# DeltaNet and SwiGLU block: shorter unread products on TensorE, and GpSimd takes part in scaling a mask and spreading Z

## The chip, the cores and the metric

The kernel runs on one core of a Trainium2 chip. Its engines are TensorE (PE, with its weight loads PEld), VectorE (DVE), ScalarE (ACT), GpSimd (POOL) and SyncE (SP, which here issues nearly all DMAs). [...] The metric is the device time of one execution in microseconds; lower is better.

## What is computed

The reference has two parts. The first is a delta-rule recurrence over 768 steps for 4 batches of 8 heads with head size 48. The second is a gated feed-forward layer on its output.

```python
k_n = k / (np.linalg.norm(k, axis=-1, keepdims=True) + 1e-06)
for t in range(S):
    kt, vt, bt = (k_n[:, :, t], v[:, :, t], beta[:, :, t, None])
    y[:, :, t] = np.einsum('bhd,bhde->bhe', q[:, :, t], state)
    v_old = np.einsum('bhde,bhd->bhe', state, kt)
    state = state + bt[:, :, :, None] * np.einsum('bhd,bhe->bhde', kt, vt - v_old)
...
x = np.ascontiguousarray(attn_out.transpose(0, 2, 1, 3)).reshape(B * S, H * D)
g = x @ w_gate
silu = g * (1.0 / (1.0 + np.exp(-g)))
val = x @ w_val
return (silu * val @ w_out).astype(np.float32)
```

w_gate and w_val are 384x1536, w_out is 1536x384; the three come in as 64-bit floats, which the kernel converts to 32 bits itself.

## The kernel before

**Chunks.** The 768 steps are cut into 12 chunks of 64. Inside a chunk the recurrence becomes products: a Gram matrix of K, a unit triangular matrix built from it and from beta, and that matrix's inverse applied to V. Then follow the output of the chunk (through a masked product of Q and K) and the new state. The feed-forward layer for a chunk runs on TensorE while the next chunk's recurrence is prepared beside it. From about 130 us on this is a steady stream of large products. The opening before it is different, since there is nothing yet to hide the recurrence behind.

**The opening.** The body of the kernel is written inside a block that fixes, for PE, ACT, DVE, SP and POOL, the order of the instructions to that in which they are written. Its first part (from L1635) is a list of calls, each of which emits instructions for several engines:

- norms(0), norms(1) on DVE, and the loads of K, Q and V by SP.
- unread(5) (L633): five products of 32 columns of weights with a moving operand of 512 columns, whose result nobody reads. A product in 32-bit floats is two passes in the trace.
- turned(0, ...) transposes K of chunk 0 through TensorE, first_gram makes its Gram matrix, first_diag copies the diagonal blocks into the tile mb on ScalarE; the same then for chunk 1.
- DVE transposes these blocks (L1655); first_scale (L679) multiplies beta and scales the 16x16 masks of both halves with it: POOL makes the factor nb, DVE multiplies the mask (L688).
- stage(n) for n = 0 to 22 fetches pieces of the weights, see below.
- first_substitution (L692): 15 steps on DVE, each a product and a sum. Step j reads row j of the mask: zb[j] times mb[j], added to the rows behind it.
- first_z (L712) transposes the result into Z. spread_z(c, x, engine, heads) (L717) copies Z of chunk c into the padded tile zt, times a mask of rows m_rows. For chunk 0 there are three such copies ahead of the next step: x = 1 for heads 0 to 7 on ScalarE, x = 0 for all heads on DVE, x = 1 for heads 8 to 15 on DVE.
- scale_v(0) and the second halves of the Q Gram steps (a mask multiplied on DVE).
- small_unread(56) (L639) and warm(1) (L646): 56 products of one column and one product of 512 columns, none of them read.
- step("advance", advance, 0): n_products(0) makes N on TensorE from zt and the lower blocks l_sb. Its products go through the heads in the order of every(): the first is of par 0, the second of par 1. A product of par 1 reads zt of heads 8 to 15. Then n_copy (ScalarE), the products p_u with V, and three rounds of correction with N.
- after that the conversion of the weights and the first feed-forward products.

**The staging of weights.** stage(n, after) emits two things. If `after` is given, POOL copies one column of piece `after` into the place of piece n. Then SP issues the DMA of piece n, which overwrites that column:

```python
if after is not None:
    nc.gpsimd.tensor_copy(place[:, 0:1], staged[after][:, 0:1])
queue.dma_start(
    out=place, in_=src[t * 128 : (t + 1) * 128, f0 : f0 + m].bitcast(U32)
)
```

So POOL's copy waits until piece `after` has landed, and SP's DMA waits for POOL's copy: only two or three pieces are under way at a time. The calls stand in this order around the spreads (L1657 to L1681):

```python
for n in range(12):
    stage(n, n - 2 if n > 1 else None)
load_v(1)
stage(12, 10)
stage(13, 11)
...
first_substitution()
for n in range(14, 18):
    stage(n, n - 3)
first_z()
for n in range(18, 23):
    stage(n, n - 3)
```

Of the kernel before, what the change touches and what calls it, by code (L numbers as in the profile page):

```python
# [10 lines left out]
ALU = mybir.AluOpType  # L11
# [4 lines left out]
R = 32  # L16
# [4 lines left out]
def kernel(  # L21
# [25 lines left out]
    nc = tc.nc  # L47
# [21 lines left out]
    def ps_pair(name, tag):  # L69

        return psum.tile([128, 2, 512], FP32, name=name, tag=tag, bufs=1)
# [70 lines left out]
    def load_k(c, dmas=(nc.sync,)):  # L142
        load_heads(kn_of(c), k, c, dmas)

    def load_q(c):
        load_heads(qpad[c % QB], q, c)
# [163 lines left out]
    half = const.tile([128, R], FP32, name="half")  # L310
# [7 lines left out]
    for b in range(2):  # L318
        rows = mask_q[64 * b : 64 * b + 64]
        nc.gpsimd.affine_select(  # L320
            out=rows,
# [35 lines left out]
    def new_n(g):  # L357

        n_t[g] = work.tile([128, 2, HH], FP32, name="n_t")
# [58 lines left out]
    def load_beta():  # L418
        for s_ in range(2):
            for par in range(2):  # L420
                at = beta_rows(s_).start + 8 * par
                nc.gpsimd.dma_start(
                    out=beta_s[at : at + 8],
                    in_=beta.rearrange(
                        "(b bp) (j par) s -> b par (bp j) s", b=2, par=2
                    )[s_ ^ par, par],
                )
# [119 lines left out]
    def gram(*args):  # L547
        for _ in gram_steps(*args):
            pass
# [51 lines left out]
    B16 = R // 2  # L601

    def pairs_of_blocks(flat):

        v = flat.rearrange("p (b n) -> p b n", b=2)[:, :, 0 : B16 * R]
        return v.rearrange("p b (k i) -> p b k i", i=R)
# [23 lines left out]
        )  # L630
        nc.vector.tensor_scalar_mul(m_low, m_rows[:, 0:3], -1.0)

    def unread(count):  # L633

        p = ps_pair("p_t", "px")[:, 0]
        for _ in range(count):
            nc.tensor.matmul(p[0:R], half, half[:, 0:1].to_broadcast([128, 512]))  # L637

    def small_unread(count):  # L639

        p = ps_pair("p_t", "px")[:, 0]
        for n in range(count):
            q_ = QUADS[n % 4][0]
            nc.tensor.matmul(p[q_, 0:1], half[q_], half[q_, 0:1])

    def warm(count):  # L646

        p = ps_pair("p_t", "px")[:, 0]
        for _ in range(count):
            nc.tensor.matmul(p, ident, kts[0][:, 0:512])  # L650
# [15 lines left out]
    def first_diag(c, p):  # L666
        to = first_of["diag"][:, HH * c : HH * c + HH]
        nc.scalar.copy(to.rearrange("p (par h) j -> p par h j", par=2), p[:, :, 1])
# [10 lines left out]
    def first_scale(r_b):  # L679
        zb, b = first_of["zb"], beta_b[:, 0]  # L680
        nb = work.tile([128, R], FP32, name="nb", tag="nb_1", bufs=1)
        for _ in range(2):
            nc.gpsimd.tensor_tensor(out=b, in0=b, in1=r_b, op=ALU.mult)
        nc.gpsimd.tensor_scalar_mul(nb, b, -1.0)
        nc.gpsimd.tensor_copy(zb[:, 0 : R * R : R + 1], b)
        mb = pairs_of_blocks(first_of["mb"])[:, :, :, 0:B16]
        nb = nb.rearrange("p (b i) -> p b i", b=2)[:, :, None, :]
        nc.vector.tensor_tensor(  # L688
            out=mb, in0=mb, in1=nb.to_broadcast([128, 2, B16, B16]), op=ALU.mult
        )  # L690

    def first_substitution():  # L692

# [23 lines left out]
    def spread_z(c, x, engine, heads=slice(0, HH)):  # L717

        z_v = first_of["z"].rearrange("p i (c h) -> p c h i", c=2)[:, c, heads]
        out = ztp[0][:, c, heads, R * x : R * x + R]  # L720
        mask = m_rows[:, 1:2] if x else m_rows[:, 3:4]
        if engine is nc.scalar:
            nc.scalar.mul(out, z_v, mask)
        else:
            nc.vector.tensor_scalar_mul(out, z_v, mask)

    def n_products(c, p_n, pars):

# [14 lines left out]
    def new_nt(c, flat):  # L743
        n_sb[c] = flat.rearrange("p (par bp j i) -> p par bp j i", bp=NB, par=2, j=NJ)
# [5 lines left out]
    QUADS = [(slice(R * n, R * n + R), R * (n % 2)) for n in range(4)]  # L750
# [875 lines left out]
    with tc.manual_schedule(  # L1626
        engines={
            mybir.EngineType.PE,
            mybir.EngineType.Activation,
            mybir.EngineType.DVE,  # L1630
            mybir.EngineType.SP,
            mybir.EngineType.Pool,
        }
    ):
        new_n(0)  # L1635
        load_beta()
        first_tiles()
        norms(0)
        norms(1)
        load_q(0)  # L1640
        load_k(2)
        load_k(3)
        load_q(1)
        load_v(0)
        copy_a = nc.scalar.copy
        unread(5)
        turned(0, False, 0)
        p_g = [first_gram(0, "px")]
        first_diag(0, p_g[0])
        turned(1, False, 2)  # L1650
        spread_beta(copy_a)
        p_g.append(first_gram(1, "py"))
        first_diag(1, p_g[1])
        r_b = first_n()
        nc.vector.transpose(first_of["mb"][:, 0 : R * R], first_of["flat"])  # L1655
        first_scale(r_b)
# [5 lines that stand above are left out]
        low_copies(0, p_g[0])  # L1662
        turned(0, True, 0)
        low_copies(1, p_g[1])
        turned(2, False, "px")
        first_q = [gram_steps(0, True, 2)]
        next(first_q[0])
        turned(3, False, "py")
        turned(1, True, 0)
        gram(2, False, "px", (copy_a, copy_a))  # L1670
        gram(3, False, "py", (copy_a, copy_a))
        first_q.append(gram_steps(1, True, 0))
        next(first_q[1])
        for n in (0, 2):
            power_step(n)
# [6 lines that stand above are left out]
        some, others = slice(0, HH // 2), slice(HH // 2, HH)  # L1682
        spread_z(0, 1, nc.scalar, some)
        spread_z(0, 0, nc.vector)
        spread_z(0, 1, nc.vector, others)
        scale_v(0)
        for steps_of in first_q:
            next(steps_of)
        small_unread(56)
        warm(1)  # L1690
        new_nt(0, qpad[1].rearrange("p bp h d -> p (bp h d)"))
        zb_1 = work.tile([128, R, R], FP32, name="zb", bufs=1)
        new_nt(1, zb_1.rearrange("p k i -> p (k i)"))
        step("advance", advance, 0)
        for x in range(2):
            spread_z(1, x, nc.scalar)
        for n in (4, 1, 3, 5, 6, 7):
            power_step(n)
        for _ in range(6):
            step("advance", advance, 0)  # L1700
        converts_first(0)
        step("advance", advance, 0)
        converts_first(2)
        p_n = banks("p_n", "px")
        n_products(1, p_n, (0,))
        step("advance", advance, 0)
        converts_first(4)
        n_products(1, p_n, (1,))
        converts_first(1, 3)
        converts_first(5)  # L1710
        scale_v(1)
        for par in range(2):
            n_copy(1, p_n, par)

        def chain(at):

            step("advance", advance, 0 if steps("advance", 0) < 4 else 1)
            converts(1 + (at + 1) % 2)

        pairs = [(c, f) for c in range(2) for f in range(0, 8, 2)]  # L1720
        pairs += [(c, f) for f in range(8, FT, 2) for c in range(2)]
        for at, (c, f) in enumerate(pairs):
            early = c == 0 and f < 4
            if c == 1 and f == 0:
                finish(1)
                second_inverse.append(invert(1))
                for _ in range(3):
                    next(second_inverse[0])
            elif not early:
                point(2)  # L1730
            need((6, 12, 18, 24, 30, 30)[f // 2])
            gate_val(c, f, fill, at, chain if early else None)
        need(len(pieces))
        for bp in range(NB):
            point(2)
            output(0, bp, fill, (4, 8))
        output(1, 0, fill, (4, 8))
        hold.clear()
        first_blocks(True)
        first_blocks(False)  # L1740
        point(2)
        output(1, 1, fill, range(2, FT, 2))
        finish(2)
        x_sums(2)
        sums_of_w(12)
        for c in range(2, NCH):
            if c > FAST:
                begin(c, 0)
            point(c + 1)
            if c == FAST:  # L1750
                begin(c, 0)
            for r in range(ROUNDS):
                gate_val_fast(c, r, fill)
            output_fast(c, fill)
            finish(c + 1)
            x_sums(c + 1)
# [30 lines left out]
```

## Time and profile before

| | |
|---|---|
| median of three runs | 697.36 us (696.71 to 699.23) |
| the profiled execution's own time | 697.91 us |
| its span | 696.2 us |
| mean granted TensorE clock | 0.994 |
| idle time of TensorE in the span | 12 us |

The profile is of one execution. A row gives the start, the busy time, the engine, the line of the kernel, the operation, what it writes and reads, and how many instructions were merged into the row. The bracket at its end is the time that the engine sat idle before it, and what ended that idle time. SPq rows are DMAs as SyncE issues them. A few stretches of the opening, as a table of busy time in us:

| us | PE | DVE | ACT | POOL | granted clock |
|---|---|---|---|---|---|
| 1.03 to 7.65 | 6.62 | 4.11 | 1.49 | 4.34 | 1.00 |
| 20 to 25 | 4.83 | 4.45 | 4.04 | 0.20 | 1.00 |
| 26 to 27 | 0.17 | 0.90 | 0.78 | 0.00 | 1.00 |
| 30 to 31 | 1.00 | 1.00 | 0.00 | 0.00 | 0.50 |
| 36 to 40 | 4.00 | 2.22 | 4.00 | 0.55 | 1.00 |
| 46 to 70 | 23.89 | 19.33 | 13.98 | 1.67 | 1.00 |

### The profile page before, as it was taken

To read this page: it belongs to the slowest core of one execution; us is meant where nothing else is said; L and a number is where in the kernel's file an instruction comes from. 1 tells how busy PE (TensorE), PEld (TensorE's weight loads), DVE (VectorE), ACT (ScalarE), POOL (GpSimd) and SP (SyncE) were. 2 spreads that over 40 slices of the span, in tenths; PEclk is the share of its full clock that TensorE was granted. 3 is DMA by queue.
4 is the path that set the end of the run, shared out by engine and by line. 5 is a ranking of instruction groups with operands and counts; after the bars stand their busy time and mean duration, and the time that the engine had idled before them with its cause. 6 is when DMAs were issued, how large, how long until landed. Compare 5 with 4: busy or idle time off the path is not lost.

```text
span 696.2 us, 25657 instructions
## 1 busy us (share of the span) xinstructions
PE 684.1 (98%) x11380; PEld 638.6 (92%) x11380; DVE 473.2 (68%) x1103; ACT 259.4 (37%) x542; POOL 53.3 (8%) x62
## 2 busy tenths in 40 slices
PE   8899999999999999999999999999999999999997
PEld 4688888757999999999999999999999999999997
DVE  6877778897899758886459786389844345333342
ACT  3675765214442532344233244242153142142230
POOL 5000031105000020000300002100000000000000
PEclk9899999999999999999999999999999999999999
DMA  9667824017450621464423373143141231121210
GB/s 133 152 166 196 256 74 154 1 38 176 126 111 13 115 80 40 102 114 85 93 72 71 70 137 70 56 108 70 55 108 48 56 84 46 55 63 46 69 47 23
DMA packets 143854, 62.31 MB, mean 90 GB/s; under 512 B 122976, under 2 KB 126048, under 8 KB 143744
## 3 DMA queue, kind: packets, MB, share of 16 engines
q1 hardware_dynamic: 141536, 60.19, 36.8%
q8 instruction: 89, 1.46, 0.8%
q10 hardware_dynamic: 2080, 0.39, 0.4%
q0 software_dynamic: 128, 0.10, 0.1%
q14 instruction: 21, 0.17, 0.1%
HBM read 53.58 MB, written 7.08 MB: 87 GB/s over the span
## 4 chain that ended last, share of the span: by engine, by line
PE 96%; ACT 1%; issue 1%; DVE 1%; ACTq 0%; DVEq 0%
PE ffn L1180 43%; PE ffn L1386 20%; PE ffn L1276 9%; PE ffn L1303 4%; PE p_g L513 3%; PE p_u L944 2%; PE p_s L1012 2%; PE p_r L905 2%; PE p_y L914 2%; PE p_y L1000 1%; PE p_f L1073 1%; PE p_t L637 1%; PE ffn L964 1%; PE p_u L964 1%; PE p_j L868 1%
## 5 line engine op out<-in xcount | busy, mean ns | idle before, releaser
L1180 PE MATMUL ffn<-x_ffn,wg_sb 128*128 128x128 f32 x840 | 128.3, 275 | 0.3 <-ACT ffn L1236 0.2
L1180 PE MATMUL ffn<-x_ffn,wv_sb 128*128 128x128 f32 x840 | 128.1, 275 | 0.0
L1180 PEld LDWEIGHTS ffn<-x_ffn,wg_sb 128*128 128x128 f32 x840 | 111.1, 192 | 0.6 <-ACT ffn L1236 0.3
L1180 PEld LDWEIGHTS ffn<-x_ffn,wv_sb 128*128 128x128 f32 x840 | 110.7, 192 | 0.0
L1210 ACT ACTIVATE sil<-ffn 128x256 f32<-128x256 f32 x120 | 46.1, 384 | 131.8 <-PE ffn L1180 127.1
L1386 PE MATMUL ffn<-wo_sb,h_f 128*128 128x192 f32 x480 | 83.4, 327 | 0.0
L1215 DVE TENSOR_TENSOR h_f<-sil,ffn 128x256 f32<-128x256 f32 x120 | 49.6, 418 | 47.6 <-ACT sil L1210 45.2
L1386 PEld LDWEIGHTS ffn<-wo_sb,h_f 128*128 128x128 f32 x480 | 78.1, 190 | 0.4
L1347 DVE TENSOR_TENSOR ffn<-ffn,p_sb 128x512 f32<-128x512 f32 x58 | 40.3, 696 | 44.3 <-ACT ffn L1236 43.2
L1180 PE MATMUL ffn<-x_t,h_f 128*128 128x128 f32 x480 | 61.1, 280 | 0.0
L1180 PEld LDWEIGHTS ffn<-x_t,h_f 128*128 128x128 f32 x480 | 56.2, 191 | 1.3 <-ACT ffn L1193 0.2
L591 DVE TENSOR_TENSOR zb<-zb,tmp 128x31 f32<-128x31 f32 (+15 forms) x155 | 53.1, 343 | 5.3
L585 DVE TENSOR_TENSOR tmp<-zb,mb 128x31 f32<-128x31 f32 (+15 forms) x155 | 52.7, 340 | 4.0
L813 POOL TENSOR_TENSOR n_b<-mb,half 128x32 f32<-128x32 f32 x5 | 30.0, 6000 | 289.8 <-DVE mb L555 289.8
L1347 DVE TENSOR_TENSOR o_sb<-o_sb,ffn 128x192 f32<-128x192 f32 x49 | 17.2, 351 | 51.1 <-PE ffn L1386 49.0
L1193 ACT COPY ffn<-ffn 128x512 f32<-128x512 f32 x30 | 17.1, 571 | 63.7 <-PE ffn L1180 57.3
L1386 PE MATMUL ffn<-last_k,h_f 128*128 128x192 f32 x200 | 35.9, 327 | 0.0
L1276 PE MATMUL ffn<-x_ffn,wg_sb 128*128 128x256 f32 x144 | 34.3, 384 | 0.0
L1276 PE MATMUL ffn<-x_ffn,wv_sb 128*128 128x256 f32 x144 | 33.8, 382 | 0.0
L1386 PEld LDWEIGHTS ffn<-last_k,h_f 128*128 128x128 f32 x200 | 32.9, 190 | 0.0
L1276 PEld LDWEIGHTS ffn<-x_ffn,wv_sb 128*128 128x128 f32 x144 | 27.0, 190 | 3.7
L1276 PEld LDWEIGHTS ffn<-x_ffn,wg_sb 128*128 128x128 f32 x144 | 26.6, 190 | 4.1 <-DVE wg_sb L304 0.4
(291 smaller groups left out, 1070.3 us busy)
## 6 DMA issues: line engine op xcount, KB each, us to landing
h_f<-w_s SPq DMA_DIRECT2D x60, 256.0 KB, 2.8
p_sb<-w_s SPq DMA_DIRECT2D x27, 256.0 KB, 2.7
vin<-in_v_dram SPq DMA_DIRECT2D x48, 96.0 KB, 3.3
out_dram<-o_sb SPq DMA_DIRECT2D x48, 96.0 KB, 2.2
kn<-in_k_dram SPq DMA_DIRECT2D x20, 192.0 KB, 4.6
zt<-in_moe_w_out_dram SPq DMA_DIRECT2D x6, 384.0 KB, 4.3
qpad<-in_q_dram SPq DMA_DIRECT2D x36, 64.0 KB, 3.2
w_s<-h_f SPq DMA_DIRECT2D x7, 256.0 KB, 3.6
```

Of the source, the lines that this page charges most:

```text
L513: nc.tensor.matmul(p_v[par][half_of(b if of_q else b ^ par), bp, j], kt[c][half_of(par), bp, j, b], xt[half_of(par), bp, j, b],)
L585: nc.vector.tensor_tensor(out=t_v, in0=zb[:, 0 : j + 1, j : j + 1].to_broadcast([128, j + 1, m]), in1=mb[:, j : j + 1, j + 1 : R].to_broad ...
L591: nc.vector.tensor_tensor(out=zb[:, 0 : j + 1, j + 1 : R], in0=zb[:, 0 : j + 1, j + 1 : R], in1=t_v, op=ALU.add,)
L813: nc.gpsimd.tensor_tensor(out=n, in0=mb.rearrange("p j i -> p (j i)")[:, 0 : R * R : R + 1], in1=half, op=ALU.pow,)
L1180: nc.tensor.matmul(p[:, u], w(u), moving, start=start and u == 0, stop=True, skip_group_check=True,)
L1193: nc.scalar.copy(p_y, p_x)
L1210: nc.scalar.activation(sil[:, n].rearrange("p (i n) -> p i n", i=2), p[:, 0:2], ACTF.Silu)
L1215: nc.vector.tensor_tensor(out=h_of(c, f, j), in0=sil[:, n].rearrange("p (i n) -> p i n", i=2), in1=p[:, 2:4], op=ALU.mult,)
L1276: nc.tensor.matmul(ps[name][:, i], w_sb[:, t, (f + i) * 128 : (f + i + 1) * 128], xts[c][:, t], start=(t == 0 and i == 0), stop=(t == KT - 1),
L1303: nc.tensor.matmul(p_o, hs[c, f - f % 2][:, f % 2, bp * 128 : (bp + 1) * 128], wo_sb[:, f], start=(f == 0), stop=(f == FT - 1),)
L1347: nc.vector.tensor_tensor(out=out, in0=a, in1=b, op=ALU.add)
L1386: nc.tensor.matmul(p[x, part], a(f - f % 2)[:, f % 2], b(f), start=not begun and f == 0, stop=f == FH - 1, skip_group_check=True,)
```

## The change

The opening's five unread products of 512 columns become three, of 512, 512 and 256 columns. The 56 unread products of one column before N go, and the warming product there becomes two. In first_scale the multiplication of the mask is cut by rows: DVE takes rows 0 to 3, GpSimd rows 4 to 15. The third spread of Z for chunk 0 (x = 1, heads 8 to 15) goes from DVE to GpSimd, at the same place of the written order.

```diff
-    def unread(count):
+    def unread(*sizes):
 
         p = ps_pair("p_t", "px")[:, 0]
-        for _ in range(count):
-            nc.tensor.matmul(p[0:R], half, half[:, 0:1].to_broadcast([128, 512]))
-
-    def small_unread(count):
-
-        p = ps_pair("p_t", "px")[:, 0]
-        for n in range(count):
-            q_ = QUADS[n % 4][0]
-            nc.tensor.matmul(p[q_, 0:1], half[q_], half[q_, 0:1])
+        for n in sizes:
+            nc.tensor.matmul(p[0:R, 0:n], half, half[:, 0:1].to_broadcast([128, n]))
...
         mb = pairs_of_blocks(first_of["mb"])[:, :, :, 0:B16]
         nb = nb.rearrange("p (b i) -> p b i", b=2)[:, :, None, :]
-        nc.vector.tensor_tensor(
-            out=mb, in0=mb, in1=nb.to_broadcast([128, 2, B16, B16]), op=ALU.mult
-        )
+        for engine, lo, hi in ((nc.vector, 0, 4), (nc.gpsimd, 4, B16)):
+            engine.tensor_tensor(
+                out=mb[:, :, lo:hi],
+                in0=mb[:, :, lo:hi],
+                in1=nb.to_broadcast([128, 2, hi - lo, B16]),
+                op=ALU.mult,
+            )
...
         if engine is nc.scalar:
             nc.scalar.mul(out, z_v, mask)
         else:
-            nc.vector.tensor_scalar_mul(out, z_v, mask)
+            engine.tensor_scalar_mul(out, z_v, mask)
...
         copy_a = nc.scalar.copy
-        unread(5)
+        unread(512, 512, 256)
         turned(0, False, 0)
...
         spread_z(0, 1, nc.scalar, some)
         spread_z(0, 0, nc.vector)
-        spread_z(0, 1, nc.vector, others)
+        spread_z(0, 1, nc.gpsimd, others)
         scale_v(0)
         for steps_of in first_q:
             next(steps_of)
-        small_unread(56)
-        warm(1)
+        warm(2)
```

## The prediction

> **What bounds the kernel now.** I read the page first. Its busy line says that TensorE sets the time; the other engines matter where TensorE waits for them.
>
> ```profile
> PE 684.1 (98%) x11380; PEld 638.6 (92%) x11380; DVE 473.2 (68%) x1103; ACT 259.4 (37%) x542; POOL 53.3 (8%) x62
> ```
>
> Of 696.2 us TensorE is idle for 12, so an edit off its path is worth nothing, and a wait put in its path costs its full length unless some of those 12 us come back. All edits lie before 31 us, so I read the chain of waits there next (start, length, what).
>
> ```profile
> 1.03 6.62 PE p_t L637 x10
> 26.17 1.49 issue
> 27.67 1.02 PE p_t L644 x82
> 28.73 1.59 PE p_t L650 x2
> 30.32 1.05 PE p_n L734 x28
> ```
>
> The chain opens with the unread products (L637), and just before the first products of N (p_n, L734) it runs through 56 small unread products (L644) and one warming product (L650, two passes). What N truly needs is the VectorE chain beside it. The timelines of VectorE, ScalarE and TensorE:
>
> ```profile
> 16.98 1.25 DVE L1655 STREAM_TRANSPOSE wo_sb<-mb 128x1024 f32<-128x1024 f32 x1 [2.27 <-ACT mb L668]
> 18.32 0.69 DVE L688 TENSOR_TENSOR wo_sb<-wo_sb,nb 128x512 f32<-128x512 f32 x1
> 27.79 1.25 DVE L714 STREAM_TRANSPOSE mb<-zt 128x1024 f32<-128x1024 f32 x1
> 29.07 1.05 DVE L725 TENSOR_SCALAR zt<-mb,m_rows 128x512 f32<-128x512 f32 x2
> 29.07 0.80 ACT L723 ACTIVATE zt<-mb,m_rows 128x256 f32<-128x256 f32 x1 [0.43 <-DVE mb L714]
> 30.25 2.49 PE L734 MATMUL p_n<-zt,a_sb 64*64 64x64 f32 x62
> ```
>
> Mask scaled (L688), 15 substitution steps, a transpose, then three spreads of Z: VectorE's end at 29.07 + 1.05 = 30.12, ScalarE's at 29.87, and N starts at 30.25.
>
> The change gives the last spread to POOL, so I asked what POOL does at 29 us. Its timeline (start, busy time, operation, idle time before it and who ended that), five of its copies of one column:
>
> ```profile
> 24.57 0.20 POOL L254 COPY h_f<-h_f 128x1 uint32<-128x1 uint32 x1 [8.55 <-DMA h_f<-in_moe_w_gate_dram]
> 29.12 0.70 POOL L254 COPY h_f<-h_f 128x1 uint32<-128x1 uint32 x1 [0.96 <-DMA h_f<-in_moe_w_val_dram]
> 43.68 0.18 POOL L254 COPY wo_sb<-wo_sb 128x1 uint32<-128x1 uint32 x1 [3.08 <-DMA wo_sb<-in_moe_w_gate_dram]
> 54.43 0.20 POOL L254 COPY wo_sb<-wo_sb 128x1 uint32<-128x1 uint32 x1 [4.27 <-DMA wo_sb<-in_moe_w_gate_dram]
> 60.21 0.18 POOL L254 COPY zt<-wo_sb 128x1 uint32<-128x1 uint32 x1 [0.98 <-DMA wo_sb<-in_moe_w_val_dram]
> ```
>
> POOL is nearly empty (8% busy) and still not free. These are the pacing copies of stage(): before piece n of the weights is fetched, POOL copies a column of piece n-2 or n-3, and so waits until that has landed. There are 21 copies (n = 2 to 22); the one at 29.12 is the fourth (n = 5), the last (n = 22) begins at 60.21. In the code all 21 stand ahead of the spreads.
>
> Is each queue worked off in the order of the code? SyncE shows it: load_v(1) is written between stage(11) and stage(12), and is issued there.
>
> ```profile
> 40.63 1.71 SPq L255 DMA_DIRECT2D zt<-in_moe_w_val_dram  x1
> 42.39 2.64 SPq L181 DMA_DIRECT2D vin<-in_v_dram  x4
> 45.13 0.57 SPq L255 DMA_DIRECT2D wo_sb<-in_moe_w_gate_dram  x1
> ```
>
> [...] the 21 copies run in their written order, each behind its own wait. [...] Here the unread passes are 0.85 us apart until 5.29 and 0.43 after it, 4.3 us after the first. [...]
>
> **The change part by part**, against the profiled execution (697.91 us, span 696.2; the median of the runs is 697.36, so 0.55 comes off at the end).
>
> *Opening products.* Ten passes of 512 columns become four of 512 and two of 256. Four cold passes take 4 x 0.85 = 3.4 us, to 4.43; two half ones 2 x 0.43 more, to 5.3. K lands by 5.78 (VectorE's first use of it), so the transposes could start near 5.85 instead of 7.58: 1.7 us earlier, and with them the Gram products, the copy that ends VectorE's wait at 16.98, and the substitution. VectorE is free from 14.70, so the gain isn't cut there. If the idle time from 5.3 to 5.85 or a late clock makes these transposes cold, 1 us of it goes (eight took 1.97 us cold at 15.80, 1.09 warm at 10.41).
>
> *Mask.* VectorE keeps 4 of 16 rows, 128 elements: 0.29 us by the L704 row of that size, instead of 0.69. POOL does 384[...]. If step 4 of the substitution is the first to wait, which comes 4 x 0.5 us on, it is hidden: gain 0.4. If step 0 waits for it, because the rows of both halves interleave in memory, the cost is 0.4 instead.
>
> *Products ahead of N.* 112 small passes and the 1.49 us idle stretch among them go; one more warming product comes: 2 passes, 0.9 us warm, 1.6 cold. Work on the second Gram matrix of Q ends at 25.95, so two warming products end by 29.2 even if cold. Between nothing and 0.1 us gained, since N waits for Z.
>
> *Z's spread.* VectorE loses 0.44 us (256 elements). POOL's price: 0.30 for 128x32, and 224 elements more at 0.84 ns (memsets: 0.95 us for 1024, 1.81 for 2048), 0.49 us. Not its price but its place decides. It stands behind stage(22)'s copy, which ends at 60.39; the spread runs from about 60.45 to 60.95, and N can start at 61.1 instead of 30.25: **+30.85 us**. TensorE needs it at once: the second product of N is of par 1, which reads just these heads. Behind that product wait all of TensorE, ScalarE (n_copy, then the weight conversions) and, after the Q masks, VectorE.
>
> Does the copies' own pace hang on the stalled engines? Pieces 0 to 22 go to places that are free by 29.04 (the last is the substitution's Z, transposed then); SyncE issues only load_v(1) and load_q(2) between them, whose buffers are free by 18 us. So there is no deadlock, and transfers alone set the pace. Nor do the gains above help: stage(0) is issued at 20.34, behind the loads on SyncE's queue, which wait for nothing on TensorE. All of them, 2 us together, are swallowed by the wait.
>
> *What is late next.* TensorE is cold after 31 us idle. N itself was already cold before (granted clock 0.5 until 32.6), 28 passes in 1.05 us, 37 ns each, against 34 warm; p_u and the first correction products would now be cold too: 0 to 2 us, I take 0.7. In return pieces 0 to 22 have landed, so ScalarE's waits for weights (1.8 us from 46 to 60, 3.0 from 60 to 82) shrink; TensorE was idle only 0.6 us from 46 to 81.6, so at most about 1 us comes back; I take 0.5.
>
> Sum: 697.91 + 30.85 + 0.7 - 0.5 = 728.96; less 0.55, 728.4, rounded to **728.5 us**.
>
> **The rivals.**
>
> 1. *The transfers run faster while the rest stands still.* The quickest pair of copies came 3.4 us apart (24.57 to 27.97). At that pace the 17 copies after 29.12 would take 29 us, so the last comes at 58, giving 726. Against more: most of it is transfer time, 256 KB each with a landing of 3.6 us, and SyncE's small-row loads stay. This end belongs to the likeliest case's range; the other end, transfers 2 us slower and 2 us of cold clock, is 732.
>
> 2. *POOL isn't held, faster.* If the spread ran on POOL at Z's arrival, beside the other two, the opening would gain 1.7, the mask 0.4 and the spread 0.3: 697.4 - 2.4 = 695.0. For it: POOL has 2 us of idle time around 30 us. Against it: the written order, which SyncE and POOL keep at every place I looked at. It decides only if POOL reaches the spread before 32 us.
>
> 3. *POOL isn't held, but its slow mask holds the substitution.* If VectorE's step 0 waits for POOL's 12 rows (0.4 lost), and the transposes run cold (0.7 gained of 1.7), while POOL's spread is no sooner than VectorE's was: 697.4 - 0.3 = 697.1, no change.
>
> **How the numbers follow.** A measurement here tells about 0.5% (3.5 us) from no change. The likeliest case, rival 1's end included: 0.94. Rival 2, at 695.0, is within the 0.5%; a little of it reaches beyond that: 0.02 faster, 0.02 same. Rival 3: 0.02. So faster 0.02, same 0.04, slower 0.94. The range is that of the likeliest case: 726 to 732 by the costs above, a us more on each side for what a second run of the same transfers does: 725 to 733.
>
> **What would show it.** A spread of 128x256 on POOL just behind its last copy of a column, near 60.5 us; p_n starting at 61 with TensorE idle from 29 or earlier, released by POOL; a granted clock of 0.5 there. The gains should still be seen ahead of it: transposes near 5.9 us, VectorE's mask at 16.6 instead of 18.3. If POOL's spread starts near 28, the forecast is wrong by its main term; if it starts at 50, the transfers were held by something that I took to be independent.

## The result

The changed kernel takes 724.75 us (723.73 to 727.05, four runs) where the kernel before takes 697.43: a ratio of 1.0376, 95% interval 1.0346 to 1.0407. The profiled execution took 723.73 us; its span is 722.0 against 696.2 before. The forecast was 728.5 with a range of 725 to 733: the cause was the forecast one, its size came out 12% smaller (27.3 us between the medians, where 31.1 were forecast), and the median lies a quarter of a microsecond below the range. Between the two profiled executions, which the account below follows, the difference is 25.8 us. What follows is mostly about those missing microseconds.

The page after, its busy line and the shares of the chain that ended last:

```profile
PE 681.5 (94%) x11266; PEld 637.9 (88%) x11266; DVE 472.4 (65%) x1102; ACT 259.8 (36%) x542; POOL 54.7 (8%) x64
...
PE 89%; DMA 5%; SPq 2%; DVE 1%; ACT 1%; issue 1%; POOL 0%; POOLq 0%; DVEq 0%; ACTq 0%
```

TensorE's work is the same but for the products taken out; its idle time has grown from 12 to 40 us, and DMAs are now 5% of the chain. POOL's timeline after, from the 4th of its copies of a column (those ahead of pieces 5 to 8, then of the last three) to the spread:

```profile
29.25 0.18 POOL L254 COPY h_f<-h_f 128x1 uint32<-128x1 uint32 x1 [0.45 <-DMA h_f<-in_moe_w_val_dram]
31.69 0.18 POOL L254 COPY h_f<-h_f 128x1 uint32<-128x1 uint32 x1 [2.26 <-DMA h_f<-in_moe_w_gate_dram]
32.29 0.18 POOL L254 COPY h_f<-h_f 128x1 uint32<-128x1 uint32 x1 [0.41 <-DMA h_f<-in_moe_w_val_dram]
34.79 0.18 POOL L254 COPY h_f<-h_f 128x1 uint32<-128x1 uint32 x1 [2.32 <-DMA h_f<-in_moe_w_gate_dram]
...
52.92 0.18 POOL L254 COPY zt<-wo_sb 128x1 uint32<-128x1 uint32 x1 [1.71 <-DMA wo_sb<-in_moe_w_val_dram]
53.84 0.18 POOL L254 COPY zt<-wo_sb 128x1 uint32<-128x1 uint32 x1 [0.73 <-DMA wo_sb<-in_moe_w_gate_dram]
54.65 0.18 POOL L254 COPY zt<-wo_sb 128x1 uint32<-128x1 uint32 x1 [0.63 <-DMA wo_sb<-in_moe_w_val_dram]
54.81 1.13 POOL L722 TENSOR_SCALAR zt<-mb,m_rows 128x256 f32<-128x256 f32 x1
```

The spread (L722) stands directly behind the copy for piece 22, as forecast, 28 us after Z was there, by VectorE's transpose:

```profile
25.72 1.25 DVE L711 STREAM_TRANSPOSE mb<-zt 128x1024 f32<-128x1024 f32 x1
```

TensorE's timeline shows who pays:

```profile
29.95 0.33 PE L731 MATMUL p_n<-zt,a_sb 64*64 64x64 f32 x2 [0.84 <-ACT zt L720]
55.99 1.87 PE L731 MATMUL p_n<-zt,a_sb 64*64 64x64 f32 x59 [25.71 <-POOL zt L722]
```

Two passes, the first product of N, run at 29.95; the next product is of par 1 and waits 25.71 us for POOL. Before, N began at 30.25. The shift is 55.99 - 30.25 = 25.74 us, and the span grew by 25.8: from there to the end it takes as long as it did (666.0 us in both).

In the forecast POOL's last copy began at 60.2, where the kernel before has it. Here it began at 54.65. At piece 5 the two traces are level (29.12 and 29.25). From there the pieces come in faster: the copies for pieces 6 and 8 are 3.10 us apart, and 4.40 in the kernel before:

```profile
31.88 0.18 POOL L254 COPY h_f<-h_f 128x1 uint32<-128x1 uint32 x1 [2.06 <-DMA h_f<-in_moe_w_gate_dram]
...
36.28 0.18 POOL L254 COPY h_f<-h_f 128x1 uint32<-128x1 uint32 x1 [3.56 <-DMA h_f<-in_moe_w_gate_dram]
```

So the question for the experiments: why does a chain of transfers that waits for no engine get faster when the engines stand still? And what are the change's other edits worth without the wait?

### The profile page after: what moved, and what is told of

The parts are those of the page before. It is cut to its first block, busy times and chain, and to the rows that moved or that the text cites. A ratio compares the mean times of both kernels' runs of the same rounds, so it can differ in the third digit from the quotient of the medians.

```text
span 722.0 us, 25429 instructions
## 1 busy us (share of the span) xinstructions
PE 681.5 (94%) x11266; PEld 637.9 (88%) x11266; DVE 472.4 (65%) x1102; ACT 259.8 (36%) x542; POOL 54.7 (8%) x64
## 3 DMA queue, kind: packets, MB, share of 16 engines
q8 instruction: 88, 1.44, 0.8%
## 4 chain that ended last, share of the span: by engine, by line
PE 89%; DMA 5%; SPq 2%; DVE 1%; ACT 1%; issue 1%; POOL 0%; POOLq 0%; DVEq 0%; ACTq 0%
PE ffn L1177 41%; PE ffn L1383 19%; PE ffn L1273 9%; PE ffn L1300 4%; PE p_g L513 2%; DMA h_f<-in_moe_w_val_dram 2%; PE p_u L941 2%; PE p_s L1009 2%; PE p_r L902 2%; PE p_y L911 1%; SPq L135 1%; PE p_y L997 1%; DMA wo_sb<-in_moe_w_val_dram 1%; PE p_u L961 1%; PE p_f L1070 1%; PE ffn L961 1%
## 5 line engine op out<-in xcount | busy, mean ns | idle before, releaser
L1177 PEld LDWEIGHTS ffn<-x_ffn,wv_sb 128*128 128x128 f32 x840 | 110.7, 192 | 0.0
L1177 PE MATMUL ffn<-x_ffn,p_sb 128*128 128x128 f32 x216 | 29.9, 282 | 0.5 <-issue 0.5
```

What stands on the lines that cost most here:

```text
L1177: nc.tensor.matmul(p[:, u], w(u), moving, start=start and u == 0, stop=True, skip_group_check=True,)
```

## Experiments: is it POOL's place, and what is the rest worth?

**Third spread back on VectorE** (z_on_vector).

```diff
-        spread_z(0, 1, nc.gpsimd, others)
+        spread_z(0, 1, nc.vector, others)
```

> The changed kernel with the third spread of Z back on VectorE; everything else of the change kept. Theory W (the whole loss is POOL's place in the written order): the loss is gone. N then starts when ScalarE's spread is done, which in the changed kernel ended at 29.90 us behind its copies of Q and its first weight conversions, so N starts near 30.0 against 30.25 before, and the time is 697.1 us, same as before within 0.5 us. Rival R (the opening's gain of 2.4 us is real once the wait is away): N near 28 us and 695 us. Rival S (something else in the change costs as well): over 700 us.

Measured: 697.45 us against 697.32 before on the same chip, ratio 0.999 (0.9968 to 1.0011). The loss is gone with this one line, and nothing is gained. The rest of the change does not help although N starts sooner, even sooner than the theory had it, at 28.71. TensorE's timeline of this run, from N to the first products with wv:

```profile
28.71 1.16 PE L731 MATMUL p_n<-zt,a_sb 64*64 64x64 f32 x64 [2.76 <-ACT zt L720]
29.69 1.77 PE L941 MATMUL p_u<-vin,zt 64*64 64x48 f32 x64
32.04 3.84 PE L961 MATMUL ffn<-v,qpad 64*64 64x48 f32 x64 [0.58 <-ACT v L950]
35.58 4.46 PE L961 MATMUL ffn<-uu,qpad 64*64 64x48 f32 x128
...
41.43 0.27 PE L731 MATMUL p_n<-zt,a_sb 64*64 64x64 f32 x2
...
49.68 1.03 PE L911 MATMUL p_y<-state,qt 64*64 64x48 f32 x57
51.78 0.33 PE L911 MATMUL p_y<-state,qt 64*64 64x48 f32 x7 [1.07 <-issue]
52.04 1.56 PE L1273 MATMUL ffn<-x_ffn,wv_sb 128*128 128x256 f32 x6
```

In the kernel before the same points lie at 30.25 (N), 36.94 (second round of correction), 42.28 (N of chunk 1) and 51.73 (wv). The lead of 1.54 us is 1.36 at the second round, 0.85 at the next N, and 0.31 us behind at the last line. Two things took it: the clock, and an idle stretch of 1.07 us in which TensorE waited for nothing that the profile shows. The clock is in the table of stretches (us, busy time and instructions, granted clock, share of the DMA engines, GB/s):

```profile
29.00:30.00 1.00, 1.00 (x80) 0.93 0.73 234
30.00:31.00 1.00, 1.00 (x48) 0.50 0.55 172
...
35.00:36.00 1.00, 1.00 (x24) 0.50 0.97 315
36.00:37.00 1.00, 1.00 (x28) 0.66 0.22 84
37.00:38.00 1.00, 1.00 (x42) 1.00 0.27 23
```

TensorE's granted clock is 0.50 until past 36 us, where the kernel before was back at 1.00 at 32.7 (0.50 in its stretch from 31 to 32, 0.66 from 32 to 33, 1.00 from 33 to 34). This is one execution of each; that the time is unchanged rests on the runs, how the lead was lost on these two traces.

**The spread alone on POOL, in the kernel before** (spread_alone).

```diff
-        spread_z(0, 1, nc.vector, others)
+        spread_z(0, 1, nc.gpsimd, others)
...
-            nc.vector.tensor_scalar_mul(out, z_v, mask)
+            engine.tensor_scalar_mul(out, z_v, mask)
```

> The kernel before with one edit: the third spread of Z goes to POOL at its place. Theory W with quick transfers (pieces land sooner because the engines stand still): POOL's last copy of a column near 54.7 us as in the changed kernel, N near 56, time 697.4 + 25.7 = 723. Rival (the transfers keep the pace of before, and it was the other edits that made them quicker): last copy near 60.2, N near 61.5, time 728 to 729.

Measured: 724.11 us, ratio 1.0371 (1.0325 to 1.0417), which is the whole loss. POOL's last copy begins at 53.94 and N resumes at 55.28. POOL's and TensorE's timelines:

```profile
53.94 0.18 POOL L254 COPY zt<-wo_sb 128x1 uint32<-128x1 uint32 x1 [0.70 <-DMA wo_sb<-in_moe_w_val_dram]
54.10 1.13 POOL L725 TENSOR_SCALAR zt<-mb,m_rows 128x256 f32<-128x256 f32 x1
```

```profile
55.28 1.88 PE L734 MATMUL p_n<-zt,a_sb 64*64 64x64 f32 x59 [25.65 <-POOL zt L725]
```

The quicker transfers come with the wait, not with the other edits. z_on_vector is the opposite case, all other edits and no wait: there the last copy begins at 58.81, and the transfers are not quicker as a whole.

**The spread ahead of the copies on POOL** (pool_spread_ahead), **and ScalarE's ahead of its conversions as well** (both_spreads_ahead). The calls that make Z move up, so that the same instructions stand elsewhere only on POOL (the lines further down from which they are taken are not shown):

```diff
-        for n in range(12):
-            stage(n, n - 2 if n > 1 else None)
+        for n in range(4):
+            stage(n, n - 2 if n > 1 else None)
+        first_substitution()
+        first_z()
+        some, others = slice(0, HH // 2), slice(HH // 2, HH)
+        spread_z(0, 1, nc.gpsimd, others)
+        for n in range(4, 12):
+            stage(n, n - 2)
         load_v(1)
```

and in both_spreads_ahead also, with the same call taken out further down,

```diff
+        spread_z(0, 1, nc.scalar, some)
         for n in (0, 2):
             power_step(n)
```

> The changed kernel with the calls for the substitution, the transpose and POOL's spread moved ahead of stage(4), so that on POOL the spread stands in front of that piece's copy; VectorE's and SyncE's orders stay. Theory W: POOL's spread runs from 27.0 to 28.1 us, no stall; N waits for ScalarE's spread and starts near 30.0; 697.1 us. Rival R: near 695. Rival: POOL's slow spread, or the piece's copy behind it, costs something: 698 to 699.

> As pool_spread_ahead, and ScalarE's spread moved ahead of its first four weight conversions. Theory: N is then held by TensorE's own warming products, which end at 29.1 us: N at 29.1 to 29.2, 1.1 us sooner than before, 696.3 us. Rival (ScalarE's spread was not what held N): no gain over pool_spread_ahead.

Measured: 699.44 us, ratio 1.0026 (1.0009 to 1.0043), and 699.06 us, 1.0024 (1.0009 to 1.0039): the stall is gone, and both are a little slower than the kernel before, so 697.1 and 696.3 were missed. The time of pool_spread_ahead is near what the last rival in its expectation had (698 to 699: the slow spread, or the piece's copy behind it, costs something). POOL's copy for piece 4 waits there for the spread, until 29.26 instead of 27.97, and its last copy begins at 61.39 instead of 60.21; that this is the cost was not tried. POOL's and then TensorE's timeline of pool_spread_ahead:

```profile
26.88 2.42 POOL L722 TENSOR_SCALAR zt<-mb,m_rows 128x256 f32<-128x256 f32 x1 [1.33 <-DVE mb L711]
29.26 0.30 POOL L254 COPY h_f<-h_f 128x1 uint32<-128x1 uint32 x2
```

```profile
27.88 2.57 PE L643 MATMUL p_t<-kt,ident 128*128 128x512 f32 x4
30.37 1.16 PE L731 MATMUL p_n<-zt,a_sb 64*64 64x64 f32 x64
```

Here POOL's spread starts when Z is there, and takes 2.42 us, with VectorE at work beside it, against 1.13 us with VectorE idle in the changed kernel; VectorE's own copy of that size took 0.44 before. N starts at 30.37, no sooner than in the kernel before: the two warming products end only there. With ScalarE's spread moved too it is 30.32, again right behind the warming products (27.32 to 30.40), so ScalarE's spread wasn't what held it. The expectation had the warming products end at 29.1.

## Experiments: why did the transfers get faster?

All runs here are the changed kernel with idle work put into the wait, at the same place and each time on another engine; the outputs of that work are not used. What is read is POOL's copies, since each starts when an earlier piece has landed.

The first four were run once each. The edits stand behind `warm(2)`; one each for tensor_long, tensor_small, vector_busy and scalar_busy, in this order:

```diff
         warm(2)
+        unread(*[512] * 26)
...
+        small_unread(560)
...
+        for _ in range(36):
+            nc.vector.tensor_tensor(
+                out=sil.rearrange("p x n -> p (x n)"),
+                in0=kts[0][:, 0:512],
+                in1=kts[1][:, 0:512],
+                op=ALU.add,
+            )
...
+        for _ in range(44):
+            nc.scalar.copy(sil.rearrange("p x n -> p (x n)"), kts[0][:, 0:512])
```

> The changed kernel with 26 more unread products of 512 columns (52 passes, 22 us) on TensorE while it waits for POOL. What is read is when POOL's last copy of a column begins: 54.7 in the changed kernel, 60.2 in the kernel before. Theory F (instruction fetches of the working engines take transfer time from the pieces): few instructions, so it stays near 54.7. Rival T (TensorE's reading of the on-chip memory slows the pieces): near 60. The time is 724 to 725 if it stays, 730 if not.

> The changed kernel with the 560 one-column unread products of the old kind on TensorE in the wait. Theory F (instruction fetches): fetches appear in the wait and POOL's last copy comes at 57 to 60. Rival T or rival V (work of VectorE or ScalarE slows the pieces): it stays near 54.7.

> The changed kernel with 36 additions of 128x512 on VectorE, some 23 us, in the wait; their result is overwritten later. Rival V: POOL's last copy comes at 57 to 60. Theory F: it stays near 54.7.

> The changed kernel with 44 copies of 128x512 on ScalarE, some 23 us, in the wait; their result is overwritten later. Rival V for ScalarE: POOL's last copy comes at 57 to 60. Theory F: it stays near 54.7.

The last column counts, in the trace's DMA records, the transfers of 16 KB on the queue of instructions (q8) that start between those two copies. The profile names that queue "instruction" (in the kernel before it moved 89 packets, 1.46 MB in all), and such a transfer is called a fetch of instructions, or a fetch, here. Each row is one execution.

| | last copy begins, us | copy for piece 6 to that for piece 22, us | fetches |
|---|---|---|---|
| before | 60.21 | 28.33 | 7 |
| z_on_vector | 58.81 | 28.21 | 6 |
| after | 54.65 | 22.96 | 0 |
| spread_alone | 53.94 | 23.47 | 0 |
| tensor_long | 56.90 | 24.29 | 0 |
| tensor_small | 57.80 | 26.46 | 7 |
| vector_busy | 55.69 | 25.21 | 0 |
| scalar_busy | 55.45 | 23.72 | 0 |

Fetches of instructions stand out, and tensor_small came out as theory F had it. But no theory has it all: with VectorE or with long products the copies are 1 to 2 us late as well, between the two expectations, though two kernels without added work differ by 0.5 among themselves. Times are of no use here: the 560 small products lasted to 61 us, beyond POOL's spread, and so held N themselves (735.35 us), and the work of VectorE and of ScalarE lasted to 58 us, beyond the spread too. The other three took 730.26, 726.16 and 727.75 beside a single run of the kernel before at 701.7. So the two suspects and their sum were timed in six runs each, with less work, all of it ended before 54 us, and the changed kernel itself beside them. small_in_wait has the first of these additions, vector_in_wait the last, all_in_wait all three:

```diff
         warm(2)
+        small_unread(420)
+        for _ in range(36):
+            nc.scalar.copy(sil.rearrange("p x n -> p (x n)"), kts[0][:, 0:512])
+        for _ in range(36):
+            nc.vector.tensor_tensor(
+                out=x_t.rearrange("p x n -> p (x n)"),
+                in0=kts[0][:, 0:384],
+                in1=kts[1][:, 0:384],
+                op=ALU.add,
+            )
```

> The changed kernel unaltered, as the yardstick for the three runs beside it: 724 to 725 us, no instruction fetch of 16 KB between 29 and 55 us, 23.0 to 23.5 us from POOL's copy for piece 6 to that for piece 22.

> The changed kernel with 420 one-column unread products on TensorE, which fill the wait to about 53 us and bring six fetches of 16 KB of instructions. Theory F (fetches slow the pieces): 0.55 us for each fetch, so the copies for pieces 6 to 22 take 26.5 us instead of 23.2, and the time is 3 us above after_again. Rival (the earlier run's late copies were its own scatter): within 1 us of after_again.

> The changed kernel with 36 additions of 128x384 on VectorE in the wait, ended by 55 us. Theory V (VectorE's work slows the pieces too): 25 us from piece 6 to piece 22 and 1.5 to 2 us above after_again. Theory F alone: within 0.7 us of after_again.

> The changed kernel with all three engines at work in the wait: the 420 small products, 36 copies of 128x512 on ScalarE and the 36 additions on VectorE. If fetches and the engines' work add up: the copies for pieces 6 to 22 take the 28.3 us of the kernel before, and the time is 5 us above after_again, 729 to 730, which is what the prediction had. Theory F alone: as small_in_wait.

| | time, us (six runs) | copy for piece 6 to that for piece 22, us | fetches |
|---|---|---|---|
| after_again | 723.43 (721.89 to 725.28) | 23.43 | 0 |
| small_in_wait | 726.71 (725.76 to 727.82) | 25.72 | 6 |
| vector_in_wait | 724.46 (723.82 to 726.18) | 23.27 | 0 |
| all_in_wait | 727.75 (726.30 to 729.94) | 26.87 | 6 |

The kernel before took 699.08 us beside them (696.27 to 703.04), with so wide a scatter that the ratios to it tell little: 1.0354 (1.0316 to 1.0392) for after_again, 1.0396 (1.0362 to 1.0431) for small_in_wait, 1.0366 (1.0332 to 1.04) for vector_in_wait, 1.0417 (1.0381 to 1.0453) for all_in_wait. The four are compared with each other. Small products alone bring 3.3 us, and their runs don't overlap with those of the unaltered kernel. VectorE's work is 1.0 us by the medians, but the runs overlap and the trace shows nothing (23.27): vector_busy's delay was not found again. All three together bring 4.3; the 28.3 us and 729 to 730 us expected of them were missed. The traffic of the queues from 29 to 53 us (packets, MB, share of 16 engines) shows what the small products add; the kernel before first, then after_again, then small_in_wait:

```profile
q1 hardware_dynamic: 5932, 3.97, 64.3%
q8 instruction: 5, 0.08, 1.6%
```

```profile
q1 hardware_dynamic: 6423, 4.85, 74.5%
```

```profile
q1 hardware_dynamic: 6057, 4.18, 64.7%
q8 instruction: 7, 0.11, 1.9%
```

The queue of instructions moves 0.1 MB where the data queue moves 4, and still the data queue moves 0.7 to 0.9 MB less in the same time. In after_again there is no line of q8. POOL's copies for pieces 7 and 8, in the same order (before, after_again, small_in_wait), show where time is taken:

```profile
32.53 0.18 POOL L254 COPY h_f<-h_f 128x1 uint32<-128x1 uint32 x1 [0.47 <-DMA h_f<-in_moe_w_val_dram]
36.28 0.18 POOL L254 COPY h_f<-h_f 128x1 uint32<-128x1 uint32 x1 [3.56 <-DMA h_f<-in_moe_w_gate_dram]
```

```profile
30.35 0.18 POOL L254 COPY h_f<-h_f 128x1 uint32<-128x1 uint32 x1 [0.43 <-DMA h_f<-in_moe_w_val_dram]
32.84 0.18 POOL L254 COPY h_f<-h_f 128x1 uint32<-128x1 uint32 x1 [2.31 <-DMA h_f<-in_moe_w_gate_dram]
```

```profile
32.58 0.18 POOL L254 COPY h_f<-h_f 128x1 uint32<-128x1 uint32 x1 [0.43 <-DMA h_f<-in_moe_w_val_dram]
35.32 0.18 POOL L254 COPY h_f<-h_f 128x1 uint32<-128x1 uint32 x1 [2.56 <-DMA h_f<-in_moe_w_gate_dram]
```

POOL's idle time ahead of the copy for piece 8 is 3.56, 2.31 and 2.56 us. In the kernel before, the trace's DMA records have one fetch of 16 KB, 1.0 to 1.5 us long, in each of the four stretches from piece 4 to piece 12: at 28.71, 33.07, 37.07 and 40.53, of 1.38, 1.53, 1.02 and 1.44 us. The copies of those stretches are 3.91, 4.40, 3.53 and 3.87 us apart; in the changed kernel, without a fetch, 3.08, 3.10, 2.99 and 3.06. The longest fetch goes with the longest delay (1.30) and the shortest with the shortest (0.54).

A fetch by itself goes with less than that. In small_in_wait each of these stretches has a fetch too (0.92 to 1.03 us long), and they took 3.49, 3.35, 3.40 and 3.49 us, where after_again had 3.13, 3.11, 3.08 and 3.03: 0.2 to 0.5 us more. In z_on_vector the four together took 13.05 us with three fetches, where the changed kernel had 12.23 with none and the kernel before 15.71 with four; it lost most of its time behind piece 12. So the fetches go with a part of the delays in the kernel before, and not with the whole. How a fetch would hold up a piece no view shows. Nor was a fetch tried without the products that it comes with: that the fetches slow the pieces, and not something else that 840 passes of small products do, is argued from the counts above. All five executions in the two tables with 6 or 7 fetches took 25.7 us or more from piece 6 to piece 22, all seven without one 25.2 or less.

Of the 4.9 us between the kernel before (28.33) and after_again (23.43), small_in_wait brings back 2.3 and all_in_wait 3.4. About 1.5 us are not accounted for: the weight conversions and the rest of the real work were not put into the wait. What all_in_wait adds to small_in_wait (1.0 us by the medians, and their runs overlap) was not traced to one engine.

## Why the prediction was right or wrong

*POOL's place in the written order: right.* The spread stands behind the copy for piece 22, TensorE's second product of N waits for it, everything behind that waits too. spread_alone has the whole loss with this edit, z_on_vector none without it.

*The pace of the transfers: wrong, and this is the step that failed.* The prediction put it so: "transfers alone set the pace", and took the last copy from the kernel before, ending at 60.39. The check on dependences was right: the pieces kept coming while TensorE stood still. What was not asked is whether the pace itself, read with all engines at work, holds when they stop. The term of 30.85 us measured 25.74. The copies began 5.56 us sooner; the spread's own price gave 0.64 back (1.13 us, not 0.49: the slope of a memset was no measure for it), and 0.2 us of allowances for waits were not needed. Rival 1 had the direction, and stopped at 3.4 us for each pair of pieces, called the quickest; the trace of before has a quicker one near the end, the copies for pieces 20 and 22 (57.44 and 60.21). The changed kernel did 3.0 to 3.1 from piece 4 to piece 12. What the runs show in place of the fixed pace: small products on TensorE, with their fetches, bring back 2.3 of 4.9 us of transfer time and 3.3 us of the kernel's time, all three engines at work 3.4 and 4.3; the rest stays open. With all_in_wait, the changed kernel at work in its wait, the time is 727.75, within the range.

*What is late next: right in its sum.* Cold clock and returned waits were put at 0.7 and -0.5; N to the end is 665.95 us before and 666.01 after. The two terms were not measured one by one. The granted clock was still 0.50 when N resumed at 55.99, as expected, 0.60 from 59 to 60 us and 1.00 from 60 us on.

*The opening: more than forecast, and covered by the wait as forecast.* TensorE's transposes start at 5.85 as expected, at a granted clock of 1.00 (eight took 1.06 us), 1.7 us sooner. The copy that ends VectorE's wait came 2.5 us sooner: 0.8 more, because a gap of 1.82 us in TensorE's second Gram products became one of 1.02. So the gain was cut at VectorE's norms after all (14.65 for the transpose, 16.98 before: 2.3 us).

*The mask: a loss, half of the dearer bound.* VectorE's part took 0.29 us, as forecast, and POOL's 1.11. What POOL would need for its 384 elements the trace of the kernel before did not show (its multiplications of two inputs there are of 128x32, 0.25 us each): that its part might be hidden, and the 0.4 lost if it is not, here and in rival 3, were the author's estimates. The first step of the substitution, which took 0.19 before, now took 0.81 and ended at 17.16, when POOL ended at 17.11:

```profile
16.35 0.81 DVE L701 TENSOR_TENSOR tmp<-zt,wo_sb 128x30 f32<-128x30 f32 x1
```

```profile
16.00 1.11 POOL L682 TENSOR_TENSOR wo_sb<-wo_sb,nb 128x384 f32<-128x384 f32 x1
```

From the start of the scaling to the end of that step it is 1.20 us, against 0.99 before: 0.2 lost where 0.4 was to be won. The trace books this as work of VectorE, not as idle time. POOL's spread, too, took longer beside work of VectorE: 2.42 us in pool_spread_ahead, and 1.64 in vector_busy with the additions of 128x512 beside it, against 1.13 with VectorE idle. Whether the step of 0.81 us was slowed by POOL's work beside it, or holds a wait that the trace hides, was not tried.

*Rival 2, the gain of 2.4 us: fell twice.* POOL was held; and without the wait the gain isn't there: z_on_vector has N 1.5 us sooner and the same time, and neither kernel with the spread moved up is faster. No version tried beats the kernel before.

## What to carry to other kernels

An engine that is 8% busy can still be the wrong place for an instruction: before giving work to it, find in its timeline which instruction stands ahead of the new one at the moment when its result is needed, and what that one waits for. A chain of transfers that waits for no engine is not thereby independent of the engines: here, when they stopped, the instruction fetches stopped too (none instead of 7), and the copies for pieces 6 to 22 took 23.0 us instead of 28.3, so the wait that was read off the old trace was too long. Where products that nobody reads are taken out, look at the granted clock behind them: in the one trace of z_on_vector, which leaves out the 56 small ones, TensorE idled 2.76 us ahead of N, and the granted clock of 0.50 lasted to 36.7 us instead of 32.7. That the missing products made it last was not tried.

## What the runs showed of the hardware

- In tensor_small the stream of one-column products on TensorE went in step with the fetches of instructions. Seven times, 128 passes took 1.88 us and were followed by 1.84 to 2.94 us in which TensorE waited for nothing shown, with one fetch of 16 KB for each such round. That the stream was bound by the fetches was not shown. Four of the rounds:

```profile
34.89 1.88 PE L644 MATMUL p_t<-half 32*32 32x1 f32 x128 [1.85 <-issue]
38.62 1.88 PE L644 MATMUL p_t<-half 32*32 32x1 f32 x128 [1.84 <-issue]
42.34 1.88 PE L644 MATMUL p_t<-half 32*32 32x1 f32 x128 [1.85 <-issue]
46.90 1.88 PE L644 MATMUL p_t<-half 32*32 32x1 f32 x128 [2.67 <-issue]
```

  In the gap of 1.49 us among the 56 small products of the kernel before TensorE waited for nothing shown either.
- A fetch of 16 KB took 0.9 to 1.5 us in the kernel before from 15 to 62 us, and 0.9 to 1.3 in small_in_wait from 29 to 53 us. A stretch of two pieces of 256 KB with a fetch in it took 0.5 to 1.3 us longer in the kernel before, where all engines work, and 0.2 to 0.5 us longer in small_in_wait, where only TensorE's small products are added.
- POOL needed 1.13 us for 256 elements times a factor for each row in the changed kernel, with VectorE idle, and for the same instruction with VectorE at work 2.42 us in pool_spread_ahead and 1.64 in vector_busy.
